# One engine more in a hand-written order: transfer issues, normalization and gate rows moved in a fused attention and expert kernel

## The chip, the cores and the metric

The kernel runs on one core of one Trainium2 chip. The time is device time in microseconds (us) of that core. The kernel before took 2181.82 us (median of three runs, 2180.48 to 2183.70).

## The reference, cut to what matters

The input `x` has 2048 rows of 512. The output is `x` plus causal sliding-window attention (32 heads of 16, window 256) of the normalized rows plus a gated sum of eight experts (512 to 1376 to 512) of the same normalized rows. All eight experts count for every row, so the selection of the top eight is only a softmax.

```python
xn = _layernorm(x, axis=-1)
# attention: q, k, v = xn @ wqkv, 32 heads of 16
mask = (idx[:, None] - idx[None, :] >= 0) & (idx[:, None] - idx[None, :] < W)   # W = 256
scores = jnp.where(mask[None, None], q @ k * Dh**-0.5, -1e9)
p = softmax(scores);  A = (p @ v) @ wo
# experts, K = E = 8
gates = softmax(xn @ w_gate)
for e in range(E):
    out = out + gates[:, e:e+1] * (silu(xn @ w1[e]) @ w2[e])
return x + A + out
```

## The kernel before, in words

Everything is fp32 in value, but TensorE multiplies fp16. So each operand is scaled and split into a high part and a low part (what the high part leaves), and each product is three matmuls: high by high, high by low, low by high (`mm3`, L147 to L149). ScalarE usually makes a high part, and VectorE or GpSimd subtracts it for the low part.

**The first stage** (about 0 to 190 us). For each of four blocks of 512 rows (`tb`): `layernorm` takes mean and variance of four tiles of 128 rows on VectorE, a root on ScalarE and a Newton step on VectorE, makes the normalized tile `xn` (L1129, on GpSimd for 14 of the 16 tiles, on VectorE for the first two), transposes it on TensorE into a PSUM bank `tp` (L1144) and splits it there: high by ScalarE (L1152), low by VectorE from PSUM (L1155), and a full fp32 copy `xfa`, `xfb` by ScalarE (L1162). `values` (products `vg`) and `queries_keys` (`qk`) multiply these with weights whose largest element is first found (`mxw` L968, a transpose `mx` and a broadcast `mb` on TensorE) and which are then scaled and split (`wv`, `wqk`). `factors_of_x` makes four sums of halves of x on GpSimd (`tt` L1197, `xsl` L1205) and stores them in DRAM (`XS`).

**The steady stage** (about 190 to 2100 us). The experts' first product is a Strassen-Winograd scheme of seven products whose operands are the seven tiles `xs` (loaded from `XS`, L489) and sums of weights (made from raw tiles `r` that are loaded at L249 and L265). TensorE writes to two pairs of PSUM banks, `zx` and `zy`; ScalarE copies `zx` out (L691), VectorE adds `zy` (`za` L698, `zb` L708). A row of the hidden layer then goes through tanh on ScalarE (L595), silu on VectorE (L599), high part on ScalarE (`hh` L610), low part on GpSimd (`hl` L613), and into the second product (`acc`). The 43 pairs of 256 hidden columns lie in 17 groups; in the group of three pairs whose columns belong to two experts each (the mixed group), the gate is multiplied in by VectorE at L605 from a tile `gb` that two transfers fill (L642, L643). There is one buffer `gb`, and each use waits for its own load.

**Attention** runs in between: 14 loads of `q` and `k` rows and one of `v` for each pair of heads (`att_load`, L1478 to L1484), scores `sc`, row maxima on VectorE (L1495, with a scratch output `junk` in SBUF), a transpose `mT`, the maxima split into `mh` and `ml` (L1520, L1523, L1526) and put into spare rows of `q` by four transfers (L1530), the scores again with the maximum subtracted (`st`, L1608), exp, masking on GpSimd, split into `ph` and `pl`, product `pv`, ratio `ot`, transpose `oT`, and the output product `wo` that VectorE adds into `x` (L1694).

**What sets the order.** The class `Order` keeps a planned clock for each of ScalarE, VectorE, GpSimd and SyncE (`"A"`, `"V"`, `"G"`, `"S"`). A `task` has a cost in ns, dependences, a due time, and a lag before its result counts. Whenever the plan's TensorE time moves on, `advance` takes the job that can start first. `Stream`s hand out pieces of TensorE work; `beside` and `wait` fill in attention (a credit of `RATE = 0.6` pieces for each piece of expert work) and second products. The instructions are then emitted in that order for the engines in `by_hand` (L210): TensorE, ScalarE, VectorE, GpSimd. SyncE, whose queue issues all transfers, is not among them: a task for it counts 50 ns in the plan, and the framework's own scheduler places its instructions. Loads of `xs` and those of `att_load` are issued where the program text reaches them, without a task.

Of the kernel before, what the change touches and what calls it, by code (L numbers as in the profile page):

```python
# [15 lines left out]
ALU = mybir.AluOpType  # L16
# [32 lines left out]
RATE = 0.6  # L49
# [5 lines left out]
LOADED = 6000  # L55
# [21 lines left out]
class Order:  # L77
# [3 lines left out]
    def __init__(self):  # L81
        self.t = 0
        self.clock = {"A": 0, "V": 0, "G": 0, "S": 0}
        self.todo = {e: [] for e in self.clock}
        self.n = 0
        self.idle = 0

# [20 lines left out]
    def advance(self):  # L108

        while True:  # L110
            best = None
            for engine, todo in self.todo.items():
                start, pick = None, None
                free = self.clock[engine]
                for job in todo:
                    e = self.at(job[5])
                    if e is None:
                        continue
                    s = max(free, e + AGO if job[5] else 0)
                    if start is None or s < start or (s == start and job[:2] < pick[:2]):  # L120
                        start, pick = s, job
# [13 lines left out]

@with_exitstack
def tile_attn_moe(ctx: ExitStack, tc: tile.TileContext, x, wqkv, wo, _bx, wg, w1, w2, out):
# [31 lines left out]
    oback = cst.tile([P, 1], F32, name="oback")  # L171
# [23 lines left out]
    by_hand = {getattr(mybir.EngineType, e) for e in ("PE", "Activation", "DVE", "Pool")}  # L195
# [98 lines left out]
    def prep1(g, i, r1, slot, act, dve, gps):  # L294
# [49 lines left out]
        w[A11] = dve(568, part(a11, 1, 0, 2), [h])  # L344
        h = act(712, part(both, 0, 6, 4), [e2])
        low = dve(831, part(both, 1, 6, 4), [h])
# [6 lines left out]
        w[S4] = w[S3] = dve(831, part(both, 1, 10, 4), [h])  # L353

    def prep2(g, i, j, r2, slot, act, dve):
# [12 lines left out]
        w["done"] = dve(898, low, [act(712, high, [])])  # L368
# [40 lines left out]
    ahead_of = {"att": 0.0, "acc": 0.0}  # L409
    bg = None  # L410
    pick = None

    def attend():
# [3 lines left out]
        for s in pick or ():  # L417
            if s.go():
# [4 lines left out]
                ahead_of["att"] += 1.0  # L423
                return True
# [31 lines left out]

    def beside(share):

        weights.go()
        ahead_of["att"] -= RATE  # L460
        while ahead_of["att"] < 0.0 and attend():
            pass
        ahead_of["acc"] -= share
        while ahead_of["acc"] < 0.0 and count[0] > hold and drain_one():
            ahead_of["att"] -= RATE
            while ahead_of["att"] < 0.0 and attend():
                pass
# [3 lines left out]
    def drain():  # L471

        wait(queue[0].needs)
        if drain_one():
            ahead_of["att"] -= RATE
            while ahead_of["att"] < 0.0 and attend():
                pass
            weights.go()

    xs = {}  # L480
    ahead = [0] * 7

    def load_x_part(m):

        if ahead[m] < len(blocks):
            b = blocks[ahead[m]]
            ahead[m] += 1
            t = moe.tile([P, 2, 2, TB // 2], F16, tag=f"xs{m}", name=f"xs{m}_{b[0]}_{b[1]}")
            nc.sync.dma_start(t, XS[b[1]][:, m])  # L489
            xs[(*b, m)] = t  # L490

    def load_xs():
        for _ in range(2):
            for m in ORDER:
                load_x_part(m)
# [13 lines left out]
    def second(g, tb, a):  # L509
# [22 lines left out]
        def add():  # L532
# [6 lines left out]
            if g == NG - 1:  # L539
                nc.sync.dma_start(o3[:, 4 * tb + a, :], dst)  # L540
            if tb == 3 and a == 3:
# [1235 lines left out]
```

## Time and profile before

| | |
|---|---|
| profiled execution | 2183.76 us, its span 2182.0 us, granted clock 0.992 |
| median of three runs | 2181.82 us |
| TensorE busy | 2121.0 us of the span, 97% |
| VectorE, ScalarE, GpSimd busy | 1764.4, 1344.8, 1104.4 us |
| transfers | 279.23 MB, 128 GB/s on average |
| hidden groups | 17, 43 pairs of 256 columns |

The span lies within the execution's time, from the first instruction to the last; 1.8 us lie around it. A row of the view of waits names the waiting engine and line and the one it waits for, then the total in us, the number of waits, and the longest. A row of the view of windows gives the stretch, its length, the busy time (and instructions) of TensorE (PE), its weight loads (PEld), VectorE (DVE), ScalarE (ACT) and GpSimd (POOL), the granted clock (PEclk), the share of the transfer engines and GB/s. SPq is SyncE's queue.

### The profile page before, as it was taken

The numbers are of one execution on the slowest core, as the hardware profiler recorded it, in microseconds if no ns is written. First come the engines' busy times: TensorE is split into PE (matmuls) and PEld (weight loads), VectorE is DVE, ScalarE is ACT, GpSimd is POOL, SyncE is SP. The second block draws the span as 40 slices with busy tenths as digits, with TensorE's granted clock in tenths as the row PEclk, the third lists the DMA queues.
The fourth block names the chain that finished last, engine by engine and source line by source line (L and its number), as shares of the span: only waits on it lengthen the run. The fifth ranks groups of instructions, "written<-read, shape, count | busy, mean of one in ns | idle before, by whom it ended". The sixth has DMA issues, their size and how long they took to land.

```text
span 2182.0 us, 46114 instructions
## 1 busy us (share of the span) xinstructions
PE 2121.0 (97%) x16519; PEld 1407.2 (64%) x16519; DVE 1764.4 (81%) x3824; ACT 1344.8 (62%) x2667; POOL 1104.4 (51%) x1624
## 2 busy tenths in 40 slices
PE   6999999999999999999999999999999999999999
PEld 4566666666666666666666666666666666666765
DVE  7767887888788888887897898789879887889762
ACT  5465665656656576566665566667666666667642
POOL 5453464545535565555444465546454546446532
PEclk9999999999999999999999999999999999999999
DMA  7856445344434444444544434353434343554111
GB/s 236 251 182 198 119 132 143 91 141 111 139 92 118 115 130 128 122 110 115 154 141 125 140 109 137 105 161 95 133 100 145 92 122 100 141 154 133 55 59 49
DMA packets 287830, 279.23 MB, mean 128 GB/s; under 512 B 128328, under 2 KB 189768, under 8 KB 287600
## 3 DMA queue, kind: packets, MB, share of 16 engines
q1 hardware_dynamic: 287600, 276.28, 43.7%
q8 instruction: 130, 2.13, 0.4%
q14 instruction: 100, 0.82, 0.1%
HBM read 250.42 MB, written 25.50 MB: 126 GB/s over the span
## 4 chain that ended last, share of the span: by engine, by line
PE 82%; DVE 7%; DMA 4%; issue 2%; POOL 2%; ACT 2%; SPq 1%; DVEq 0%; ACTq 0%; POOLq 0%
PE acc L147 12%; PE acc L149 12%; PE acc L148 12%; PE zx L147 6%; PE zx L149 6%; PE zx L148 6%; PE zy L147 5%; PE zy L149 4%; PE zy L148 4%; PE st L1608 3%; PE sc L1507 3%; PE pv L1639 3%; PE qk L1250 2%; PE vg L1305 2%; DMA gb<-GT 1%
## 5 line engine op out<-in xcount | busy, mean ns | idle before, releaser
L613 POOL TENSOR_TENSOR hl<-t,hh 128x512 f16<-128x512 f32 x344 | 431.5, 1262 | 289.0 <-ACT hh L610 269.1
L147 PE MATMUL acc<-w,hh 128*128 128x512 f16 x1376 | 523.0, 380 | 1.1 <-DVE x L535 1.1
L149 PE MATMUL acc<-w,hl 128*128 128x512 f16 x1376 | 522.8, 380 | 0.3 <-POOL hl L613 0.3
L148 PE MATMUL acc<-w,hh 128*128 128x512 f16 x1376 | 522.8, 380 | 0.0
L1569 ACT ACTIVATE pf<-st,esc 128x384 f32<-128x384 f32 (+2 forms) x576 | 299.4, 522 | 235.0 <-PE st L1608 220.2
L1553 POOL TENSOR_SCALAR_AFFINE_SELECT pf<-pf 128x128 f32<-128x128 f32 x512 | 204.8, 402 | 389.5 <-ACT pf L1569 360.3
L1579 DVE TENSOR_TENSOR pl<-pf,ph 128x384 f16<-128x384 f32 (+2 forms) x576 | 361.8, 636 | 43.7 <-ACT ph L1575 41.9
L147 PE MATMUL zx<-xs,w 128*128 128x256 f16 x1376 | 376.0, 273 | 9.3 <-DVE za L698 9.2
L149 PE MATMUL zx<-xs,w 128*128 128x256 f16 x1376 | 376.2, 273 | 0.0
L148 PE MATMUL zx<-xs,w 128*128 128x256 f16 x1376 | 376.2, 273 | 0.0
L1575 ACT ACTIVATE ph<-pf 128x384 f16<-128x384 f32 (+2 forms) x576 | 264.1, 464 | 84.2 <-POOL pf L1560 57.4
L147 PEld LDWEIGHTS <-w 128*128 128x128 f16 x2408 | 235.4, 98 | 122.0 <-DVE za L698 2.8
L148 PEld LDWEIGHTS <-w 128*128 128x128 f16 x2408 | 235.7, 98 | 106.7 <-issue 18.1
L1495 DVE CUSTOM_DVE_ANT_0 junk<-sc,mask 128x320 bf16<-128x320 f32 (+4 forms) x512 | 237.1, 463 | 78.4 <-PE sc L1507 69.6
L147 PE MATMUL zy<-xs,w 128*128 128x256 f16 x1032 | 281.3, 273 | 7.2 <-DVE zb L708 4.2
L149 PE MATMUL zy<-xs,w 128*128 128x256 f16 x1032 | 281.5, 273 | 0.0
L148 PE MATMUL zy<-xs,w 128*128 128x256 f16 x1032 | 281.3, 273 | 0.0
L610 ACT ACTIVATE hh<-t 128x512 f16<-128x512 f32 x344 | 214.2, 624 | 77.4 <-DVE t L599 49.8
L149 PEld LDWEIGHTS <-w 128*128 128x128 f16 x2408 | 235.9, 98 | 28.0
L535 DVE SCALAR_TENSOR_TENSOR x<-acc,gsc,x 128x512 f32<-128x512 f32 x256 | 190.2, 743 | 73.0 <-PE acc L149 71.7
L149 PEld LDWEIGHTS <-hl 128*128 128x128 f16 x1376 | 134.6, 98 | 164.6 <-issue 2.1
L712 POOL TENSOR_TENSOR zb<-zb 128x512 f32<-128x512 f32 x86 | 112.4, 1306 | 205.6 <-ACT zb L691 151.5
(145 smaller groups left out, 3769.3 us busy)
## 6 DMA issues: line engine op xcount, KB each, us to landing
xs<-XS SPq DMA_DIRECT2D x476, 256.0 KB
r<-in_B_w_dram SPq DMA_DIRECT2D x172, 256.0 KB
r<-in_B_w_dram SPq DMA_DIRECT2D x80, 512.0 KB
q<-QS SPq DMA_DIRECT2D x192, 32.0 KB
VS<-vt SPq DMA_DIRECT2D x16, 272.0 KB
out_dram<-x SPq DMA_DIRECT2D x16, 256.0 KB
k<-KS SPq DMA_DIRECT2D x96, 40.0 KB
x<-in_A_x_dram SPq DMA_DIRECT2D x3, 1024.0 KB
```

The source lines that it names most:

```text
L147: nc.tensor.matmul(ps, lhsT=lh, rhs=rh, start=first, stop=False, **kw)
L148: nc.tensor.matmul(ps, lhsT=lh, rhs=rl, start=False, stop=False, **kw)
L149: nc.tensor.matmul(ps, lhsT=ll, rhs=rh, start=False, stop=last, **kw)
L535: nc.vector.scalar_tensor_tensor(out=dst, in0=ps, scalar=back if groups[g][0] is None else back[:, 4 * tb + a : 4 * tb + a + 1], in1=dst, ...
L610: nc.scalar.activation(out=h["hi"], in_=h["t"], func=AF.Copy)
L613: nc.gpsimd.tensor_tensor(out=h["lo"], in0=h["t"], in1=h["hi"], op=ALU.subtract)
L712: nc.gpsimd.tensor_tensor(out=zb[:, :, late], in0=zb[:, :, early], in1=zb[:, :, late], op=ALU.add)
L1495: nc.vector.tensor_tensor_reduce(out=junk[:, :n], in0=ps[:, :n], in1=maskf[:, MB * 64 - n :], scale=1.0, scalar=-3.0e38, op0=ALU.add, op1= ...
L1553: nc.gpsimd.affine_select(out=pf[:, :P], in_=pf[:, :P], pattern=[[1, P]], channel_multiplier=-1, base=0, compare_op=ALU.is_ge, fill=0.0,)
L1569: nc.scalar.activation(out=w["pf"][:, :n], in_=ps[:, :n], func=AF.Exp, bias=math.log(PSCALE), scale=esc)
L1575: nc.scalar.activation(out=w["hi"][:, :n], in_=w["pf"][:, :n], func=AF.Copy)
L1579: nc.vector.tensor_tensor(out=w["lo"][:, :n], in0=w["pf"][:, :n], in1=w["hi"][:, :n], op=ALU.subtract)
```

## The change

What it does, part by part:

1. SyncE joins the engines whose order is written out. Each transfer is charged 450 ns of SyncE's planned time (`ISSUE`), results count 2.2 us later (`MOVED`) or 4.5 us later (`LOADED`, before 6 us). Loads of `xs`, `q`, `k`, `v`, `wo`, `gb` and `r`, the puts of `mh` and `ml` and the stores become moves with due times; products wait in the plan for their `xs` load, and `pv` alone waits for `v`. Several planned costs are set anew, the planner may prefer an earlier-due job that can start a little later until the first values are done, and attention's pace is what is left of it over what is left of the expert work.
2. Normalization: all 16 `xn` on VectorE; the low parts of x on GpSimd, from the fp32 copy in SBUF; the variance step goes (its constant is a bias of the root), the Newton step takes four instructions, not five.
3. The values' weights are loaded, searched for the largest element, scaled and split in two halves; the second half's low part is made on GpSimd after a second ScalarE pass. Products start with high by high as soon as high parts stand, and up to three product groups are open at once.
4. Two buffers `gb`. To make room, the mask is bf16, the row maxima's scratch output goes back into the PSUM bank it was read from, and `nm` goes (`mh` and `ml` are made from PSUM by two instructions, not three).

The matmuls are the same (16,500 in place of 16,498 TensorE instructions of the program).

Three places show how instructions stand on their queues. The first is SyncE's queue in the mixed group (`gb` gate rows, `q`, `k` attention rows, number suffixes are the buffer). Before:

```order
L1478 DMA k_94<-KS 16x1280 x2
L1530 DMA q_96<-mh 1x16x64
L1530 DMA q_96<-ml 1x16x64
L1530 DMA q_96<-mh 1x16x64
L1530 DMA q_96<-ml 1x16x64
L642 DMA gb<-GT 96x512
L643 DMA gb<-GT 32x512
L1478 DMA k_94<-KS 16x1280
```

After:

```order
L1611 DMA q_92<-mh 1x16x64
L1611 DMA q_92<-ml 1x16x64
L1611 DMA q_92<-mh 1x16x64
L1611 DMA q_92<-ml 1x16x64
L664 DMA gb<-GT 64x512
L665 DMA gb<-GT 64x512
L664 DMA gb<-GT 32x512
L665 DMA gb<-GT 96x512
L1746 DMA wo<-WOS 128x1024
```

Two gate rows now stand one behind the other; the four puts of `mh` and `ml` still stand ahead of them.

The second is SyncE's queue where the first raw tiles of group 5 (`r_5_0`, `r_5_1`) are loaded, beside a pair of heads' loads. Before:

```order
L1482 DMA q_92<-ZERO 2x16x64
L1484 DMA v<-VS 128x8x68
L489 DMA xs_4_0_8605<-XS_61 128x1024
L265 DMA r_5_0_8640<-in_B_w_dram 128x512 x2
L489 DMA xs_4_0_8654<-XS_61 128x1024
```

After:

```order
L280 DMA r_5_0_8417<-in_B_w_dram 128x512 x2
L512 DMA xs_4_0_8448<-XS_61 128x1024
L512 DMA xs_4_0_8486<-XS_61 128x1024
L512 DMA xs_4_1_8554<-XS_62 128x1024
L280 DMA r_5_1_8571<-in_B_w_dram 128x512 x2
L512 DMA xs_4_1_8614<-XS_62 128x1024
L1611 DMA q_96<-mh 1x16x64
L1611 DMA q_96<-ml 1x16x64
L1611 DMA q_96<-mh 1x16x64
L1611 DMA q_96<-ml 1x16x64
L135 DMA k_94<-KS 16x1024
```

The raw tiles stood behind the fifteen loads of the pair of heads (the last two of them shown) and now stand ahead of them.

The third is GpSimd's queue in the first stage. Before:

```order
L1197 TENSOR_TENSOR tt<-xfb,xfa 128x512
L1205 TENSOR_TENSOR xsl<-tt,xsh 128x512
L1197 TENSOR_TENSOR tt<-xfb,tt 128x512
L1129 TENSOR_SCALAR xn<-x_133,mv,rs 128x512
L1205 TENSOR_TENSOR xsl<-tt,xsh 128x512
L1129 TENSOR_SCALAR xn<-x_133,mv,rs 128x512 x3
L1197 TENSOR_TENSOR tt<-xfa 128x512
```

After:

```order
L1236 TENSOR_TENSOR tt<-xfb,xfa 128x512
L1244 TENSOR_TENSOR xsl<-tt,xsh 128x512
L1236 TENSOR_TENSOR tt<-xfb,tt 128x512
L1244 TENSOR_TENSOR xsl<-tt,xsh 128x512
L1193 TENSOR_TENSOR x_453<-xfa,x_451 128x2x128
L1193 TENSOR_TENSOR x_454<-xfb,x_452 128x2x128
```

The normalization (L1129) is gone from the queue, and the low parts of x (L1193, eight for each block of rows) stand in it, behind the sums of the block before.

The diff's core:

```diff
-RATE = 0.6
+AFTER = 80
+ISSUE = 450
-LOADED = 6000
+LOADED = 4500
+MOVED = 2200
@@ class Order, advance
+                    soon = [c for c in can if c[1:3] < (due, n) and c[0] < start + pick[2] // 2]
+                    if soon and self.strict:
+                        start, due, n, pick = min(soon, key=lambda c: c[1:3])
+    def issued(self, n, after=0):
+        self.clock["S"] = max(self.clock["S"], after) + n * ISSUE
+        return Event(self.clock["S"] + MOVED)
+
+    def move(self, n, run, deps, slack, lag=MOVED):
+        return self.task("S", n * ISSUE, run, deps, slack, lag)
@@ tile_attn_moe
-    by_hand = {getattr(mybir.EngineType, e) for e in ("PE", "Activation", "DVE", "Pool")}
+    by_hand = {getattr(mybir.EngineType, e) for e in ("PE", "Activation", "DVE", "Pool", "SP")}
@@ attention's pace
-        ahead_of["att"] -= RATE
+        left["groups"] -= 1
+        ahead_of["att"] -= left["att"] / max(left["groups"] - AFTER, 1)
@@ load_x_part (the moves of xs)
-            nc.sync.dma_start(t, XS[b[1]][:, m])
-            xs[(*b, m)] = t
+            def run():
+                t = moe.tile([P, 2, 2, TB // 2], F16, tag=f"xs{m}", name=f"xs{m}_{b[0]}_{b[1]}")
+                nc.sync.dma_start(t, XS[b[1]][:, m])
+                xs[(*b, m)] = t
+            xs_at[(*b, m)] = order.move(1, run, free + (...), slack, LOADED)
@@ row, gate_rows
-            ld = order.task("S", 50, gate_load, [last_gate], slack, 3000)
-            s = last_gate = order.task("V", 693, gate, [s, ld], slack + 4000)
+            ld = order.move(2, gate_load, [gated_at[0]], slack - 3000, LOADED)
+            s = order.task("V", 706, gate, [s, ld], slack + 4000)
+            gated_at[:] = [gated_at[-1], All([s, ld])]
-        t = at.tile([P, TB], F32, tag="gb", bufs=1, name="gb")
+        t = at.tile([P, TB], F32, tag="gb", bufs=2, name="gb")
@@ loaded (raw tiles r)
-            ev = order.task("S", 50, run, [lambda: order.at(raw_gone[which]), *deps], due, LOADED)
+            n = 4 if which == 1 and groups[g][0] is None else which
+            ev = order.move(n, run, [lambda: order.at(raw_gone[which]), *deps], due, LOADED)
@@ layernorm
-                    (nc.gpsimd if on_pool else nc.vector).tensor_scalar(
+                    nc.vector.tensor_scalar(
                         out=box["xn"], in0=xa[:, i, :], scalar1=mv[:, i, 0:1], scalar2=rs[:, i, :],
                         op0=ALU.subtract, op1=ALU.mult,
                     )
-                    nc.vector.scalar_tensor_tensor(
-                        out=xl[c][:, :, ts], in0=half[c], scalar=SX, in1=xh[c][:, :, ts], op0=ALU.mult, op1=ALU.subtract
-                    )
+                    nc.gpsimd.tensor_tensor(out=xl[c][:, :, ts], in0=xf[c][:, :, ts], in1=xh[c][:, :, ts], op=ALU.subtract)
@@ weights of values, second half (of == 4)
+                if of == 4:
+                    return t, task("G", 1270, rest, [task("A", cost, scaled, [t], slack + more + 500)], slack + more)
@@ go_on
-                if any(s.go() for s in sides) or main.go():
+                if any(s.go() for s in sides) or any(s.go() for s in mains[:3]):
@@ att_load
-                nc.sync.dma_start(kf[part, : s.nk], KS[r // 2, rows, s.k0 : s.k0 + s.nk])
+                move(kf[part, : s.nk], KS[r // 2, rows, s.k0 : s.k0 + s.nk])
-        s.loaded = Event(order.t + LOADED)
+        s.loaded = All(parts)
+        s.v_at = order.move(1, values, free, 8000)
@@ att_max
-    mask = att.tile([P, MB, 64], F32, name="mask")
+    mask = att.tile([P, MB, 64], BF16, name="mask")
-                out=junk[:, :n], in0=ps[:, :n], in1=maskf[:, MB * 64 - n :], scale=1.0, scalar=-3.0e38,
+                out=ps[:, :n], in0=ps[:, :n], in1=maskf[:, MB * 64 - n :], scale=1.0, scalar=-3.0e38,
-        s.ready = order.task("V", 356, low, [t], 2000, LOADED // 2)
+        s.ready = order.move(5, put, [t], 0)
```

More of the change, by code (lines that the diff above doesn't have):

```diff
@@ L366, in low @@
             )
-        w["done"] = dve(898, low, [act(712, high, [])])
+        w["done"] = dve(838, low, [act(712, high, [])])
     doubles = []
@@ L409, in tile_attn_moe @@
     ahead_of = {"att": 0.0, "acc": 0.0}
+    left = {
+        "att": sum(H // 2 * (2 * (min(hf, 1) * WIN + HALF) // P + QB + 2 * QB + 1) for hf in range(2)) + H // 8 * 2 * 10,
+        "groups": 14 * ND + 4 * 4 * 2 * sum(len(pairs) for _, pairs in groups),
+    }
     bg = None
@@ L487, in load_x_part @@
             ahead[m] += 1
-            t = moe.tile([P, 2, 2, TB // 2], F16, tag=f"xs{m}", name=f"xs{m}_{b[0]}_{b[1]}")
-            nc.sync.dma_start(t, XS[b[1]][:, m])
-            xs[(*b, m)] = t
[L492 to L495, printed above, removed]
+            def run():
+                t = moe.tile([P, 2, 2, TB // 2], F16, tag=f"xs{m}", name=f"xs{m}_{b[0]}_{b[1]}")
+                nc.sync.dma_start(t, XS[b[1]][:, m])
+                xs[(*b, m)] = t
+            xs_at[(*b, m)] = order.move(1, run, free + ([xs_at[(*blocks[ahead[m] - 2], m)]] if ahead[m] > 1 else []), slack, LOADED)
     def made_of(ws, of, what):
@@ L540, in add @@
                 nc.sync.dma_start(o3[:, 4 * tb + a, :], dst)
+                order.issued(1, order.clock["V"] + 746)
             if tb == 3 and a == 3:
@@ L995, in top @@
             def top():
+                if m == 2:
+                    topped.end = order.clock["V"] + 560
                 if n == 1:
@@ new lines, in layernorm @@
+                if i == 0 or (i < 3 and tb == 0):
+                    m = slice(i, i + 1 if tb == 0 and i < 2 else 4)
+                    turn = [] if tb else [Event(0), topped, found[2], found[2]]
+                    t = [
+                        task("V", 860, partial(stats, j), [x_at[tb][j], *turn[j : j + 1]], slack + less)
+                        for j in range(m.start, m.stop)
+                    ]
+                    t = task("A", 250 if tb == 0 else 1500, partial(root, m), t, slack)
+                    t = task("V", 650 if m.stop - m.start == 1 else 1000, partial(newton, m), [t], slack + less - 8000 * (m.stop == 4))
@@ L1207, in low @@
                     nc.sync.dma_start(XS[tb][:, m, 1], box["lo"])
+                    order.issued(2, order.clock["G"] + 1220)
                 deps = [made[x1]] if x1 in (T1, T2) else []
@@ L1288, in tile_attn_moe @@
+                if beside:
+                    t = order.task("A", 600, high, [ev, stored[j]], 4000)
+                    stored[j] = Event()
+                    evicted[j] = order.task("V", 690, low, [t], 5000)
+                else:
+                    place[j] = task("V", 690, low, [task("A", 600, high, [ev], 5000)], 6000)
+            return [Lazy(partial(group, w, c)) for w in ws for c in range(4)]
         vt4 = p0.tile([P, 4, H, VC], F16, name="vt")
@@ L1335, in gate @@
+            turns = [(i, hv) for i in range(4) for hv in range(2)]
+            if tb == 0:
+                turns[1:3] = turns[2], turns[1]
+            return [Lazy(partial(group, i, hv)) for i, hv in turns]
         def gate(tb, lg, logits):
@@ L1472, in att_load, with move @@
         qf, kf = s.q, s.k
+        free = [Event(order.t + DRAIN)]
+        parts = []
+        def move(dst, src):
+            parts.append(order.move(1, partial(nc.sync.dma_start, dst, src), free, 4000))
         for a in range(2):
@@ L1660, in att_wo, with load @@
         nonlocal oh_gone
-        wt = at.tile([P, 2, D], F16, tag="wo", bufs=1, name="wo")
-        nc.sync.dma_start(wt, WOS[qd])
-        loaded = Event(order.t + LOADED)
+        wt = []
+        def load():
+            wt.append(at.tile([P, 2, D], F16, tag="wo", bufs=1, name="wo"))
+            nc.sync.dma_start(wt[0], WOS[qd])
+        loaded = order.move(1, load, [oh_gone], 4000, LOADED)
         for jh in range(2):
```

478 lines of the change are left out of this document (248 added, 230 removed).

## The prediction

> **What bounds the kernel now.** I read the busy times first, then the windows by stage, then TensorE's waits, then the timeline around the longest ones.
>
> ```profile
> PE 2121.0 (97%) x16519; PEld 1407.2 (64%) x16519; DVE 1764.4 (81%) x3824; ACT 1344.8 (62%) x2667; POOL 1104.4 (51%) x1624
> ```
>
> TensorE bounds: it is busy 2121.0 us of 2182.0, and the change takes no matmul away. So at most 61.0 us of its idle time can be won, and what it runs at a lower clock. The windows say where (length, then PE, PEld, DVE, ACT, POOL busy, clock, DMA share, GB/s):
>
> ```profile
> 0.00:30.00 30.00, 15.54 (x77) 10.81 (x77) 19.60 (x64) 11.11 (x31) 14.53 (x20) 0.89 0.78 249
> 30.00:130.00 100.00, 88.54 (x478) 48.38 (x476) 72.28 (x170) 55.49 (x133) 54.13 (x38) 0.95 0.70 216
> 130.00:190.00 60.00, 60.00 (x438) 42.51 (x437) 38.30 (x94) 31.51 (x73) 19.12 (x19) 1.00 0.67 211
> 190.00:2100.00 1910.00, 1878.76 (x15050) 1258.32 (x15049) 1605.48 (x3459) 1224.77 (x2396) 999.01 (x1532) 1.00 0.43 123
> 2100.00:2182.00 82.00, 78.19 (x483) 47.14 (x481) 28.78 (x40) 21.93 (x36) 17.58 (x15) 1.00 0.11 42
> ```
>
> Idle is 14.5 us before 30, 11.5 from 30 to 130, 31.2 in the steady stage, 3.8 in the last. Below full clock:
>
> ```profile
> 21.00:28.00 7.00, 5.89 (x27) 4.07 (x26) 3.28 (x11) 4.17 (x14) 3.67 (x3) 0.51 0.73 214
> 52.00:59.00 7.00, 6.04 (x18) 3.02 (x19) 4.71 (x11) 3.76 (x9) 2.02 (x1) 0.52 0.71 201
> 83.00:86.00 3.00, 3.00 (x9) 1.08 (x8) 1.11 (x2) 1.30 (x5) 1.81 (x2) 0.50 0.90 284
> 359.00:363.00 4.00, 4.00 (x19) 2.29 (x18) 0.63 (x1) 2.30 (x5) 2.06 (x7) 0.57 0.96 319
> 601.00:608.00 7.00, 5.50 (x24) 3.01 (x24) 5.43 (x15) 3.62 (x7) 1.69 (x3) 0.53 0.38 130
> 1182.00:1185.00 3.00, 2.90 (x10) 1.43 (x10) 2.65 (x5) 2.63 (x6) 1.82 (x4) 0.50 0.77 130
> 1253.00:1256.00 3.00, 3.00 (x14) 1.61 (x13) 3.00 (x5) 2.18 (x5) 3.00 (x4) 0.57 0.35 85
> ```
>
> Busy time by one minus the clock is what they cost: 2.9, 2.9 and 1.5 us in the first stage (7.3); 1.7, 2.6, 1.5 and 1.3 in the steady one (7.1). With the idle time that makes 75 us, the ceiling. TensorE's waits (total, times, longest):
>
> ```profile
> PE tp L1144 <- POOL xn L1129: 11.8, 10, 2.5
> PE zx L147 <- DVE za L698: 9.2, 6, 3.8
> PE mx L992 <- DVE mx L979: 9.2, 1, 9.2
> PE st L1608 <- DMA q<-ml: 6.9, 9, 3.2
> PE zy L147 <- DVE zb L708: 4.2, 2, 3.9
> PE zy L147 <- DVE za L698: 2.7, 4, 1.6
> PE tp L1144 <- DVE xn L1129: 2.3, 1, 2.3
> PE vg L1305 <- ACT wv L1021: 1.8, 1, 1.8
> ```
>
> The first stage waits for normalized tiles, the steady one for VectorE's `za` and `zb` (16.1 us) and for puts of the maxima (6.9 us).
>
> **First stage, the start.**
>
> ```profile
> 7.58 1.27 DVE L968 TENSOR_REDUCE mxw<-wraw 128x1 f32<-128x512 f32 x2
> 12.98 5.24 PE L1305 MATMUL vg<-wv,x 128*128 128x260 f16 x24 [1.81 <-ACT wv L1021]
> 20.56 0.66 PE L1144 MATMUL tp<-ident,xn 128*128 128x128 f32 x4 [2.33 <-DVE xn L1129]
> ```
>
> Halving the values' weights takes two of the four reductions (1.3 us for two) from the way of the first `mx`. The waits of 1.8 and 2.3 us behind it should shrink with the new order; I take half, 2.0. Together −3.3. Bounds: all of the 5.4 us and the 2.9 of low clock (−8.3); and +2 if the second half's extra passes (a ScalarE pass like `wv` and a GpSimd pass of 1.26 us like `hl`, both quoted next) get in front.
>
> **First stage, normalization and low parts.**
>
> ```profile
> L1129 POOL TENSOR_SCALAR xn<-x,mv,rs 128x512 f32<-128x512 f32 x14 | 29.3, 2099 | 13.6 <-DVE rs L1114 11.2 <-PE qk L1250 1.7 <-issue 0.8
> L1129 DVE TENSOR_SCALAR xn<-x,mv,rs 128x512 f32<-128x512 f32 x2 | 1.2, 585 | 0.0
> L1155 DVE SCALAR_TENSOR_TENSOR x<-tp,x 128x256 f16<-128x256 f32 x32 | 12.0, 417 | 5.3 <-ACT x L1152 3.6 <-ACT xfa L1162 1.2 <-ACT xfb L1162 0.5
> L324 POOL TENSOR_TENSOR sums<-r 128x256 f32<-128x256 f32 x43 | 34.9, 811 | 16.3 <-DMA r<-in_B_w_dram 11.6 <-DVE w L309 4.7
> L613 POOL TENSOR_TENSOR hl<-t,hh 128x512 f16<-128x512 f32 x344 | 431.5, 1262 | 289.0 <-ACT hh L610 269.1 <-PE acc L149 3.9 <-DMA xs<-XS 3.2
> L1021 ACT ACTIVATE wv<-wraw,sc 128x512 f16<-128x512 f32 x4 | 2.6, 707 | 0.0
> ```
>
> A tile's normalization falls from 2.10 to 0.585 us, and it no longer stands behind the sums in GpSimd's queue. VectorE gains 14 × 0.585 = 8.2 us and loses the low parts' 12.0. GpSimd loses 29.3 us and gains 32 low parts: between 0.63 us (half of `hl`) and 0.81 us (`sums`, the same size), 20 to 26 us; I take 0.81, plus 2.5 for the second half's weights. So neither engine is fuller. The low parts come later (0.81 for 0.417 us, behind two ScalarE copies), but a product group now begins with high by high. Of the 11.8 us of `tp` waits I take 7.5 away (about two thirds), and of the 4.4 us of low clock behind them half, 2.2: −9.7. Bounds: −16 and 0. First stage: **−13**.
>
> One sentence on a rule: the Trainium skill (TensorE: Matmul & The Clock Gate, "What's actually happening") halves the clock after an idle window of about 3.4 us; the 0.52 at 52 to 59, with no single `tp` wait over 2.5 us, shows that several shorter waits do it too, so by the page alone the 2.2 us would be nothing and the forecast 2 us higher.
>
> **Steady stage, gate rows.**
>
> ```profile
> 1174.98 0.52 SPq L642 DMA_DIRECT2D gb<-GT  x1
> 1179.95 0.69 DVE L605 TENSOR_TENSOR t<-t,gb 128x512 f32<-128x512 f32 x1 [4.65 <-DMA gb<-GT]
> 1182.10 0.37 PE L147 MATMUL zx<-xs,w 128*128 128x256 f16 x1 [3.41 <-DVE za L698]
> ```
>
> The window of the mixed group:
>
> ```profile
> 1110.00:1270.00 160.00, 149.70 (x1173) 99.68 (x1171) 133.60 (x277) 96.71 (x191) 77.59 (x119) 0.98 0.46 134
> ```
>
> One buffer: the load goes out only after the gate before, 5.0 us from issue to use; VectorE stands, its `za` behind it is late, TensorE stands 3.4 us and then runs at 0.50. The mixed group holds 24 gates in 160 us, one in 6.7 us, so a load issued one gate earlier covers 5 us. Of its 10.3 us of idle I take 9. Bounds −10.3 and 0 (the four puts still stand ahead).
>
> **Steady stage, raw tiles, puts, clock.**
>
> ```profile
> 593.65 0.85 SPq L265 DMA_DIRECT2D r<-in_B_w_dram  x2
> 600.02 1.22 DVE L804 TENSOR_REDUCE mp<-r 128x1 f32<-128x1024 f32 x1 [6.27 <-DMA r<-in_B_w_dram]
> ```
>
> The tile landed 6.4 us after its issue, behind a pair of heads' fifteen loads that the plan did not charge, and VectorE, in order, stood before its `za`. Now the plan charges them, and the load goes ahead. The `za` and `zb` waits outside the mixed group are 16.1 less some 9, 7.2 us: I take 4. The puts are planned 4.45 us ahead of `st` (five issues of 0.45 and 2.2), in place of 3: of 6.9 us I take 4. Of the low clock, that after 601, 1182 and 1253 (5.4 us) goes with its stalls: 5. Each is bounded by the whole of its row and nothing. Together with the gates **−22**. For waits that a new order brings in places I cannot see I add **+4**, an eighth of today's 31.2 us (bounds 0 and 31).
>
> **SyncE's order.** Written out, SyncE issues nothing earlier than planned, and what it waits for holds all that stands behind it:
>
> ```profile
> SPq L489 <- PE zx L149: 272.7, 114, 9.1
> ```
>
> That is SyncE standing before an `xs` load until its buffer is read, up to 9.1 us, with raw tiles, `q` rows and gate rows queued behind it. Before, such a load stood where the program reached it; now it is placed by due time after the product that frees its buffer is planned, so I expect this row to shrink, and count no gain for it beyond the rows above: the DMA share is 0.43 in the steady stage, so a load that is issued in time is there in time. Splitting `att_load` into fifteen moves adds no transfer; its cover is that scores start only after the plan has the last `q` and `k` row, with expert products in between. If that cover is gone, `st` or `sc` wait like the 6.9 us of `q<-ml` today; this lies in the +4.
>
> **At nothing.** The variance step, one Newton instruction and `nm` go: a few short VectorE instructions for each tile or pair of heads, hidden where VectorE is not what TensorE waits for. The bf16 mask and the two columns of `oback` change no instruction's size. The attention's pace alters which work fills the gaps, not how much there is; TensorE was full in the windows 130 to 190 and nearly so at the end, and its price would show as idle time in the last window (3.8 us today).
>
> **Maxima into PSUM.**
>
> ```profile
> L1495 DVE CUSTOM_DVE_ANT_0 junk<-sc,mask 128x320 bf16<-128x320 f32 x448 | 216.6, 484 | 64.9 <-PE sc L1507 57.5 <-DVE mt L1495 0.5
> L804 DVE TENSOR_REDUCE mp<-r 128x1 f32<-128x1024 f32 x86 | 103.6, 1207 | 17.3 <-DMA r<-in_B_w_dram 17.3
> ```
>
> No row shows VectorE writing PSUM. The upper bound is a second pass at 1.18 ns an element (1207 over 1024): 0.377 us more on 448 operations, 169 us of VectorE. The lower is a little below nothing. I take nothing, since the operation already reads that bank at 1.5 ns an element. VectorE has 305 us free in the steady stage, which hides a few us, not 169.
>
> **The sum.** 2183.8 (the profiled execution) −13 −22 +4 = 2152.8; the median lies 1.9 below that execution, so **2151 us**.
>
> **The rivals.**
> - *The steady waits only move.* One SyncE queue still carries everything in order, and a due time set wrong holds back all behind it. For it: `q<-ml` and `gb` queue behind other issues today. Against: each named wait has its own remedy. 2183.8 − 13 − 1.9 = 2169.
> - *GpSimd's low parts take the place of its normalization.* TensorE then waits for x's low parts and the first stage gives nothing: 2183.8 − 22 + 4 − 1.9 = 2164. For it: 0.81 against 0.417 us, behind the sums. Against: 54.13 of 100 us busy there, and high by high first. The Trainium skill (GPSIMD Engine Reference, "Engine selection") speaks against this move, about two times slower for two inputs on GpSimd, and these rows agree.
> - *Slower: VectorE becomes the bound.* If the maxima cost the upper bound, VectorE's free time falls from 305 to 135 us, and TensorE's waits for it with their low clock (16.1 + 7.1 = 23.2 us) grow by 2.25 to 52: 2183.8 + 29 − 13 − 1.9 = 2198. The steady remedies then find no free VectorE. It decides from about 110 us more on VectorE (0.25 us an operation), where 23.2 × (305/195 − 1) = 13 eats the first stage's gain. Against: the operation reads PSUM already.
>
> **How the numbers follow.** Forecast 0.62 (own range 2136 to 2164), moved waits 0.18, low parts 0.12, VectorE 0.08. The range 2126 to 2176 leaves out VectorE's case, the upper end of the moved waits and a gain beyond every middle value: about 2 in 10. What this kernel's measurement can tell from no change is 0.2%, 4.4 us: faster 0.86 (0.62, and most of the two middle rivals), same 0.05, slower 0.09.
>
> **What would show it.** Right: `tp` waits for xn under 4 us; no VectorE wait for `gb` over 2 us; clock 1.00 from 1100 to 1300; raw tiles that land before their reduction; `sc` maxima still near 484 ns. Wrong: waits of `vg` or `qk` for GpSimd's low parts; waits for `xs` loads; VectorE over 1700 us in the steady stage; and, for the new pace, attention left over when the expert work ends, so that the last window has TensorE idle well over 3.8 us.

## The result, and the profile after

The changed kernel took 2143.45 us (median of four runs, 2141.19 to 2145.47) against 2181.65 us for the kernel before: a ratio of 0.9824 (95% interval 0.9807 to 0.9841), 38 us less. The forecast was 2151 us. Its profiled execution took 2145.47 us, its span 2143.8, the granted clock 0.998.

The busy times and then the windows by stage of the changed kernel (stretch, length, PE, PEld, DVE, ACT, POOL busy, clock, DMA share, GB/s):

```profile
PE 2106.5 (98%) x16522; PEld 1403.6 (65%) x16522; DVE 1745.8 (81%) x3775; ACT 1348.3 (63%) x2670; POOL 1109.4 (52%) x1644
```

```profile
0.00:30.00 30.00, 17.47 (x117) 12.81 (x118) 22.48 (x70) 15.94 (x42) 18.06 (x28) 1.00 0.53 163
30.00:130.00 100.00, 93.39 (x534) 53.47 (x532) 73.44 (x156) 56.16 (x140) 49.51 (x53) 0.97 0.75 241
130.00:190.00 60.00, 54.66 (x384) 37.48 (x382) 37.47 (x89) 29.41 (x64) 17.66 (x19) 0.97 0.69 212
190.00:2100.00 1910.00, 1901.49 (x15293) 1280.83 (x15292) 1595.71 (x3436) 1239.97 (x2416) 1019.14 (x1543) 1.00 0.43 123
```

TensorE's idle time went from 61.0 us (2182.0 − 2121.0) to 37.3 (2143.8 − 2106.5), 23.7 of the 38.2 us of span; its busy time fell by 14.5 us with the same large matmuls (16,522 TensorE records in place of 16,519). About 10 us of that is low clock that went: it had cost 14.4 us by the prediction's rows, and the changed kernel still loses some 4.7 us to it, since the view of windows shows 0.86 from 30 to 50 us, 0.94 from 50 to 60 and 0.83 from 170 to 180. The rest of the 14.5 us is not traced. In the steady window idle time fell from 31.2 to 8.5 us and the clock shows 1.00. From 130 to 190 us, where TensorE had been full, it now idles 5.3 us.

TensorE's waits in the changed kernel:

```profile
PE tp L1180 <- DVE xn L1165: 12.3, 5, 7.8
PE sc L1588 <- DMA q<-ZERO: 4.7, 1, 4.7
PE vg L1353 <- ACT wv L1057: 2.6, 2, 2.0
PE sc L1588 <- ACT ph L1656: 2.1, 2, 1.2
PE sc L1588 <- DVE mt L1576: 1.8, 2, 1.1
PE zy L162 <- DVE zb L730: 1.6, 2, 1.2
PE zy L162 <- DVE za L720: 1.4, 2, 1.1
```

The largest row is now mostly the program's start (7.8 us before the first transpose, which stands where the first `mx` stood). The waits for `za` and `zb` are 3.2 us in place of 16.1, and `q<-ml` is gone. One wait is new: 4.7 us of `sc` for `q` rows, which ends just before the 0.83 of 170 to 180. On VectorE the two waits for transfers shrank, from 17.3 and 16.4 us to:

```profile
DVE mp L827 <- DMA r<-in_B_w_dram: 5.3, 3, 2.8
DVE t L626 <- DMA gb<-GT: 3.1, 4, 1.3
```

Of the 5.3 us for raw tiles all but 0.3 lie before 165 us.

For the experiments one measure is worked out from each trace's matmul records: the start of a matmul less the time that all matmuls before it take at the usual (median) start-to-start of their shape in that trace. It counts idle time and low clock together, and it is comparable at equal times although the order differs. It is a rough measure: grouping the shapes in other ways moves a whole row by up to 4 us and a difference between two rows by about 1 us. "Lost" below is this, in us, at six points:

| kernel | at 30 | at 165 | at 200 | at 1000 | at 1400 | at 2100 |
|---|---|---|---|---|---|---|
| before | 21.0 | 38.9 | 40.8 | 62.9 | 81.8 | 88.1 |
| changed | 17.0 | 28.1 | 35.6 | 43.6 | 48.6 | 50.5 |
| changed, SyncE not written | 17.4 | 24.5 | 26.8 | 30.3 | 33.0 | 34.0 |
| not written, uncharged | 16.8 | 20.6 | 28.4 | 41.6 | 66.0 | 80.2 |
| one gate buffer | 15.6 | 24.5 | 32.1 | 39.2 | 67.1 | 71.5 |
| one gate buffer, not written | 17.6 | 24.9 | 27.1 | 30.5 | 56.8 | 59.8 |
| gate buffers alone | 21.7 | 39.9 | 41.9 | 57.4 | 71.4 | 77.2 |
| normalization on GpSimd | 21.1 | 33.0 | 44.5 | 52.6 | 59.9 | 66.8 |

By it the change saved 10.8 us up to 165 us, gave 5.6 us back between 165 and 200 (7.5 lost there in place of 1.9), and saved 32.4 us from 200 to 2100 (14.9 in place of 47.3).

### The profile page after: what moved, and what is told of

It is laid out like the page before. It is cut to its first block, busy times and chain, and to the rows that moved or that the text cites. A ratio compares the mean times of both kernels' runs of the same rounds, so it can differ in the third digit from the quotient of the medians.

```text
span 2143.8 us, 45614 instructions
## 1 busy us (share of the span) xinstructions
PE 2106.5 (98%) x16522; PEld 1403.6 (65%) x16522; DVE 1745.8 (81%) x3775; ACT 1348.3 (63%) x2670; POOL 1109.4 (52%) x1644
## 4 chain that ended last, share of the span: by engine, by line
PE 90%; DVE 4%; DMA 2%; ACT 1%; issue 1%; SPq 1%; POOL 1%; DVEq 0%; POOLq 0%; ACTq 0%
PE acc L162 13%; PE acc L163 13%; PE acc L164 13%; PE zx L162 6%; PE zx L163 6%; PE zx L164 6%; PE zy L162 5%; PE zy L164 5%; PE zy L163 5%; PE st L1689 3%; PE pv L1720 3%; PE sc L1588 3%; PE qk L1291 3%; PE vg L1353 2%; PE wo L164 1%
## 5 line engine op out<-in xcount | busy, mean ns | idle before, releaser
L1634 POOL TENSOR_SCALAR_AFFINE_SELECT pf<-pf 128x128 f32<-128x128 f32 x512 | 204.6, 402 | 440.7 <-ACT pf L1650 408.4
L1660 DVE TENSOR_TENSOR pl<-pf,ph 128x384 f16<-128x384 f32 (+2 forms) x576 | 354.5, 623 | 50.7 <-ACT ph L1656 48.8
L1576 DVE CUSTOM_DVE_ANT_0 sc<-sc,mask 128x320 f32<-128x320 f32 (+4 forms) x512 | 240.0, 473 | 101.9 <-PE sc L1588 98.9
L1641 POOL TENSOR_SCALAR_AFFINE_SELECT pf<-pf 128x128 f32<-128x128 f32 x448 | 176.0, 397 | 33.3 <-ACT pf L1650 32.7
```

What stands on the lines that cost most here:

```text
L1576: nc.vector.tensor_tensor_reduce(out=ps[:, :n], in0=ps[:, :n], in1=maskf[:, MB * 64 - n :], scale=1.0, scalar=-3.0e38, op0=ALU.add, op1=AL ...
L1634: nc.gpsimd.affine_select(out=pf[:, :P], in_=pf[:, :P], pattern=[[1, P]], channel_multiplier=-1, base=0, compare_op=ALU.is_ge, fill=0.0,)
L1641: nc.gpsimd.affine_select(out=pf[:, n - P : n], in_=pf[:, n - P : n], pattern=[[-1, P]], channel_multiplier=1, base=-1, compare_op=ALU.is_ ...
L1660: nc.vector.tensor_tensor(out=w["lo"][:, :n], in0=w["pf"][:, :n], in1=w["hi"][:, :n], op=ALU.subtract)
```

## The experiments

All times below are medians beside runs of the kernel before on the same chip; each says its ratio to before.

**1. Is it the written SyncE order, or the charge?** SyncE's queue is put back under the framework's scheduler, with the plan left as it is. The other four engines' instructions stand in exactly the order of the changed kernel; only SyncE's differ.

```diff
-    by_hand = {... for e in ("PE", "Activation", "DVE", "Pool", "SP")}
+    by_hand = {... for e in ("PE", "Activation", "DVE", "Pool")}
```

> The changed kernel with SyncE taken out of the engines whose order is written; the plan still charges 450 ns for an issue, so the other engines' order is the same. Theory (SyncE's order itself carries the raw tiles and the puts): their waits come back, TensorE loses 10 to 18 us: 2153 to 2162. Rival 1 (the charge in the plan is enough, since the other engines leave the room): within 4 us of 2143.5. Rival 2 (the whole steady gain is the written order): 2170 or more.

Measured: 2128.37 us, ratio 0.9756 (0.9741 to 0.9770). Neither the theory nor its rivals had this: without the written order the kernel is 15 us faster than the changed one. VectorE's waits for transfers behind the program's start, then GpSimd's for raw tiles, in this kernel:

```profile
DVE t L626 <- DMA gb<-GT: 2.5, 2, 1.7
DVE gs L1426 <- DMA QS<-qkh: 1.7, 1, 1.7
DVE mp L827 <- DMA r<-in_B_w_dram: 0.5, 1, 0.5
```

```profile
POOL sums L339 <- DMA r<-in_B_w_dram: 11.4, 6, 5.0
```

and GpSimd's in the changed kernel:

```profile
POOL sums L339 <- DMA r<-in_B_w_dram: 39.1, 15, 10.7
```

The view also puts one wait of 10.8 us of `xsl` in the kernel without the written order down to these transfers; `xsl` reads no raw tile, so it is left out here. So raw tiles land later, against what waits for them, under the written order; the control of experiment 4 shows the same, 49.5 us written and 15.7 not. What SyncE stood for, first in the changed kernel, then without the written order:

```profile
SPq L512 <- PE zx L164: 302.1, 105, 22.3
SPq L512 <- PE sc L1588: 215.8, 80, 7.2
SPq L512 <- PE zy L164: 176.8, 86, 5.9
SPq L512 <- PE st L1689: 155.0, 69, 23.9
```

```profile
SPq L512 <- PE zx L164: 237.5, 111, 10.3
SPq L512 <- PE sc L1588: 201.0, 80, 8.0
SPq L512 <- PE zy L164: 134.1, 77, 4.3
SPq L512 <- PE st L1689: 130.7, 74, 11.6
```

These are `xs` loads that wait for their buffer: 850 us standing in place of 703. One place in the changed kernel shows what stands behind them:

```profile
933.23 7.56 SPq L512 DMA_DIRECT2D xs<-XS  x5
940.88 0.39 SPq L264 DMA_DIRECT2D r<-in_B_w_dram  x1
```

```profile
946.78 0.94 POOL L339 TENSOR_TENSOR sums<-r 128x256 f32<-128x256 f32 x1 [3.33 <-DMA r<-in_B_w_dram]
```

The five `xs` issues themselves take 0.32 us each; the rest of the 7.56 us is standing until buffers are free. A raw tile is issued only behind them, and GpSimd waits 3.3 us for it. Where the 15 us lie: at 200 us the loss is 26.8 in place of 35.6 (8.8 us, of which 5.2 between 165 and 200, at the new wait for `q` rows), and from 200 to 2100 it is 7.2 in place of 14.9 (7.7 us). Late raw tiles behind standing `xs` loads can stand for the 7.7 us at most, and that they make all of it is argued, not shown.

**2. Is the charge needed?** An issue is charged 25 ns in the plan in place of 450, once with SyncE's order written and once not.

```diff
-ISSUE = 450
+ISSUE = 25
```

> The changed kernel with an issue charged 25 ns in place of 450, SyncE's order still written. Theory (the charge is what moves raw tiles and puts ahead): VectorE's wait for raw tiles and the wait of st for the puts come back in part, 6 to 14 us: 2150 to 2158. Rival (the written order with landing times is enough): within 4 us of 2143.5.

> SyncE's order not written and an issue charged 25 ns in place of 450; all else as changed. It stands beside the run with SyncE not written but charged (2128.4 us) and the run written but uncharged (2234.5). Theory (the charge itself pays: it tells the order of the other engines when a load is there): much of the loss stays, 2160 us or more. Rival (the charge matters only because the written SyncE order is derived from it): within 5 us of 2128.

Measured: 2234.48 us written (ratio 1.0244, 1.0229 to 1.0260) and 2175.02 us not written (0.9979, 0.9969 to 0.9989). With the two runs above:

| | issues charged 450 ns | charged 25 ns |
|---|---|---|
| SyncE's order written | 2143.5 | 2234.5 |
| not written | 2128.4 | 2175.0 |

The charge is worth 47 us even where the framework places SyncE's issues, far more than the 3 us that the control of experiment 4 moves there. Without it VectorE stands for raw tiles again (0.5 us with the charge):

```profile
DVE mp L827 <- DMA r<-in_B_w_dram: 37.2, 15, 5.2
```

Which order carries the 47 us is not shown: between these two kernels the instructions of all five engines, SyncE's too, stand in other orders. By the table 24.4 us of loss lie between 1000 and 1400 us without the charge, where the charged kernel loses 2.7; the mixed group runs there. Written and uncharged, the kernel is slower than before; VectorE then waits for raw tiles and TensorE for `q` rows:

```profile
DVE mp L827 <- DMA r<-in_B_w_dram: 64.1, 17, 7.8
```

```profile
PE sc L1588 <- DMA q<-ZERO: 23.6, 6, 7.1
```

The theory of the first run had the direction and a size of 6 to 14 us; it was far too small. That of the second held (2160 us or more).

**3. The new wait at attention's start.** The loads of the first pair of heads, which the changed kernel issues back to back from 159 us on, are put into the order ahead of the last block's queries.

```diff
+        first_rows = att_rows(0, 0)
         go_on(queries_keys(3, (0,)), sides)
...
-        s = att_load(*todo[0])
+        s = att_values(first_rows)
```

> The changed kernel, SyncE's order written, with the fourteen q and k loads of the first pair of heads put into the order before the last block's queries instead of after everything of the first stage. Theory (the 4.7 us wait of sc for q at 165 us is those loads issued back to back when attention starts): that wait falls under 1 us, 2137 to 2140. Rival (the loads then stand ahead of stores and raw tiles that the first products need, and the wait moves): within 2 us of 2143.5.

Measured: 2149.00 us, ratio 0.9855 (0.9841 to 0.9870), 5.6 us slower than the changed kernel. The wait became smaller, and another one is new:

```profile
PE zx L162 <- ACT za L713: 2.9, 1, 2.9
PE sc L1597 <- DMA q<-ZERO: 2.9, 1, 2.9
```

The theory fell. The loads now begin at 147 us in place of 159, the wait ends at 161 us in place of 170, and the loss at 200 us, worked out as in the table, is that of the changed kernel within 0.1 us. The new wait of `zx` stands far from there, between 1100 and 1200 us. So the 5.6 us arise after 200 us, and they are less than what the control of experiment 4 moves: they say nothing about the loads. In the run without the written order the same loads begin 23 us earlier, at 136 us, spread among the stores, and the wait is gone (lost from 165 to 200: 2.3 us). SyncE's timeline of that run, the first row:

```profile
136.31 1.46 SPq L135 DMA_DIRECT2D k<-KS  x1
```

So the wait depends on where SyncE's issues stand, and moving the whole block did not mend it.

**4. How much does any reordering move?** A control: attention's pace a little different. And the pace as before.

```diff
-AFTER = 80
+AFTER = 90
```

```diff
-        ahead_of["att"] -= left["att"] / max(left["groups"] - AFTER, 1)
+        ahead_of["att"] -= 0.6
```

> The changed kernel with AFTER 90 in place of 80, a small change of attention's pace that nobody would expect to matter: the control for how far any reordering moves the time. Theory (the steady stage is robust once issues are charged): within 4 us of 2143.5. Rival (each order is a draw, and single draws differ by 10 us and more, so that the losses with the old pace and with one gate buffer say little by themselves): more than 6 us away, up or down.

> The changed kernel with attention's pace as before, 0.6 pieces for each piece of expert work. Theory (the waits, not the pace): 0 to +3 us, 2143 to 2147. Rival (an even pace is what relieves VectorE where attention and experts crowd): 8 to 15 us back, 2151 to 2159, with VectorE-caused waits of zx and zy over 8 us in place of 3.2.

> SyncE's order not written, issues charged, and AFTER 90 as in the control, which took 2155.1 us with SyncE's order written. The order of the other four engines is that of the control. Theory (the written SyncE order is what makes an ordering of the others cheap or dear): within 5 us of 2128.4. Rival (the order of the other engines is the draw): the control's 11.7 us stay, 2137 to 2143.

Measured: the control 2155.14 us (0.9884, 0.9870 to 0.9899), the old pace 2157.43 us (0.9888, 0.9873 to 0.9903), and the control without the written SyncE order 2131.36 us (0.9772, 0.9758 to 0.9787). So a change that should not matter costs 11.7 us with SyncE's order written and 3.0 us without. The rival held for the written order: one draw of it says nothing below about 12 us, and the 14 us of the old pace are little evidence on the pace. Without it the same reordering of the other engines stays within 3 us; on this pair the fragile part is SyncE's written queue. That the written queue costs time is no single draw: in all four pairs of runs in which only SyncE's instructions stand in another order, the kernel without the written order is the faster one, by 15.1 us (changed), 23.8 (control), 14.3 (one gate buffer, experiment 5) and 59.5 (uncharged).

**5. Gate buffers.** One buffer in the changed kernel (with the plan told so), the same without SyncE's order written, and the two buffers alone, with what makes room for them, in the kernel before.

```diff
-        t = at.tile([P, TB], F32, tag="gb", bufs=2, name="gb")
+        t = at.tile([P, TB], F32, tag="gb", bufs=1, name="gb")
-            gated_at[:] = [gated_at[-1], All([s, ld])]
+            gated_at[:] = [All([s, ld])] * 2
```

> The changed kernel with one buffer of gate rows again (in the plan too); all else as changed, 2143.5 us. Theory (each wait of the steady stage had its own remedy): VectorE's wait for gate rows comes back to 12 to 17 us from 3.1, TensorE loses 7 to 11 us in the mixed group, clock dips there again: 2150 to 2155. Rival (the written order of SyncE places the gate loads well enough with one buffer): within 3 us of 2143.5.

> One buffer of gate rows, SyncE's order not written; the other four engines in the order of the run with one gate buffer (2175.4 us, of which 28 us in the mixed group). It stands beside 2128.4 us with two buffers. Theory (with one buffer the charged plan itself orders the mixed group badly, since each gate then counts over 5 us of waiting): the loss stays on the other engines' order, 2152 to 2160. Rival 1 (the two buffers alone are worth what they gave the kernel before, 9 us, and the rest of the 32 came from the written SyncE order): 2135 to 2141.

> The kernel before with two buffers of gate rows and what makes room for them (bf16 mask, maxima's scratch output in PSUM, two instructions for the parts of the maxima); nothing else of the change. Theory (each wait had its own remedy): the mixed group's 10 us go, 2168 to 2174. Rival (the gain in the mixed group needs the charged plan, which knows what a gate row's load costs): 2176 to 2184.

Measured: 2175.42 us (0.9976, 0.9964 to 0.9987), 2161.12 us (0.9906, 0.9887 to 0.9926) and 2172.50 us (0.9962, 0.9948 to 0.9976). In the kernel before, the two buffers and what makes room for them gave about 9 us, the size forecast for that step; in the window of its mixed group TensorE's idle time went from 10.3 to 3.5 us:

```profile
1110.00:1270.00 160.00, 156.51 (x1223) 104.02 (x1222) 139.10 (x288) 99.51 (x197) 89.20 (x123) 0.98 0.50 140
```

Not all of the 9 us is the gates', though. By the table this kernel loses 10.9 us less than the kernel before up to 2100 us: 4.9 of them between 1000 and 1400, where the mixed group runs, and 6.6 between 200 and 1000, where no gate is multiplied in. What gives the 6.6 us there is not shown.

In the changed kernel going back to one buffer cost 32 us, three times as much, and 33 us without the written order, where the control moved 3, so it is not the control's kind of draw. The table puts it between 1000 and 1400 us: 27.9 lost in place of 5.0, and 26.3 in place of 2.7. The wait for the gate row itself is only 3 us larger, 6.2 us in the kernel with one buffer in place of 3.1 (the theory wanted 12 to 17):

```profile
DVE t L626 <- DMA gb<-GT: 6.2, 5, 3.5
```

The loss is idle time of TensorE and, not much less, low clock. From 1000 to 1400 us it idles 14.4 us and runs at 0.97 (some 11.6 us), where the changed kernel idles 3.1 us at 1.00; first the kernel with one buffer, then the changed one:

```profile
1000.00:1400.00 400.00, 385.61 (x2962) 255.36 (x2961) 326.17 (x672) 244.08 (x472) 199.33 (x298) 0.97 0.45 131
1000.00:1400.00 400.00, 396.95 (x3183) 268.83 (x3180) 350.65 (x719) 266.18 (x521) 223.28 (x329) 1.00 0.49 138
```

The idle time is spread over many waits; the two longest of TensorE in its window 1080 to 1320 are

```profile
PE wo L162 <- DVE x L1779: 4.0, 1, 4.0
PE acc L162 <- ACT hh L631: 2.7, 1, 2.7
```

With one buffer the plan counts 0.9 + 4.5 us from gate to gate and lays out the mixed group around that; the theory of the second run, that the loss sits in the other engines' order, held (its forecast of 2152 to 2160 was missed by 1 us: 2161). Which of their instructions carries it is not shown. The 33 us and the 47 us of the charge do not add up: together they are more than the 53 us between the kernel before and the best one. Of the loss that each brings back without the written order, 23.6 and 21.7 us lie between 1000 and 1400 us: where the mixed group runs, nearly the same is lost without the second buffer as without the charge.

**6. The maxima's scratch output.** Without the written SyncE order, the scratch goes to SBUF again. The order on the other engines is the same.

```diff
+            junk = at.tile([P, MB * 64], BF16, tag="junk", bufs=1, name="junk")
-                out=ps[:, :n], in0=ps[:, :n], ...
+                out=junk[:, :n], in0=ps[:, :n], ...
```

> SyncE's order not written (2128.4 us), and the row maxima's scratch output goes to a bf16 tile in SBUF again; room for it comes from one tile for the two parts of the maxima. Every engine but SyncE has the same order. The operation should fall from 0.494 to 0.484 us and the read of its accumulator from 0.139 to 0.081, some 35 us less of VectorE. Theory (VectorE is not the bound, its free time hides it): within 3 us of 2128.4. Rival (VectorE is near the bound, as the slower case of the forecast had it): 2118 to 2124.

Measured: 2130.61 us (0.9767, 0.9752 to 0.9781), 2.2 us from 2128.4: no difference. The groups with the output in PSUM (the kernel with SyncE not written, first) and in SBUF:

```profile
L1576 DVE CUSTOM_DVE_ANT_0 sc<-sc,mask 128x320 f32<-128x320 f32 x448 | 219.9, 495 | 86.6 <-PE sc L1588 83.5
L1576 DVE DVE_READ_ACCUMULATOR2_ANT mt<- 128x1 f32 x512 | 71.5, 140 | 0.0
```

```profile
L1577 DVE CUSTOM_DVE_ANT_0 junk<-sc,mask 128x320 bf16<-128x320 f32 x448 | 216.8, 484 | 88.6 <-PE sc L1589 81.8
L1577 DVE DVE_READ_ACCUMULATOR2_ANT mt<- 128x1 f32 x512 | 41.2, 80 | 0.0
```

**7. Normalization.** 14 of the 16 tiles on GpSimd again, the low parts of x left there too.

```diff
-                    nc.vector.tensor_scalar(
+                    (nc.gpsimd if tb > 0 or i > 1 else nc.vector).tensor_scalar(
```

> The changed kernel with 14 of the 16 normalizations on GpSimd again, low parts of x also on GpSimd. Theory (the first stage gained because tiles no longer wait for GpSimd): waits of tp for xn come back to 10 us or more, GpSimd now has 29 us more than in the changed kernel, 2152 to 2160. Rival (high by high first and several open groups hide it): within 4 us of 2143.5.

Measured: 2160.60 us, ratio 0.9908 (0.9893 to 0.9922), 17 us slower than the changed kernel, close to the forecast in size, but not at the place named. The waits of `tp` for GpSimd came back only as

```profile
PE tp L1180 <- POOL xn L1165: 2.6, 3, 1.4
```

which is less than the 4.5 us that `tp` waits for VectorE in the changed kernel beside the program's start (12.3 less 7.8). So it is not shown that the move to VectorE took the waits for normalized tiles away (14.1 us before, 11.8 and 2.3). The rival that the run names, high by high first and several open groups, is still possible for these waits; it was not tried apart, and in this run TensorE also stood elsewhere, which can hide them. Against the changed kernel, 4.9 us more were lost up to 165, 4.0 more up to 200 and 7.4 after. In the first part stand waits that the changed kernel does not have: 3.5 us of `mb` for the largest weight at 85 us, 1.6 us of `qk` for `wqk` at 50 us, and 2.6 us of `zx` at 159 us. Since this was run with SyncE's order written, where the control moved 12 us, the rest is open.

## Why the prediction held, step by step

- **First stage, −13.** The start of the changed kernel's timeline stands below. Measured −10.8 up to 165 us in the changed kernel, and −14.4 without the written SyncE order (24.5 against 38.9). The step was right in sum, but neither of its two reasons is borne out. The start was wrong: first `vg` at 12.65 us in place of 12.98, so halving the weights did not bring it forward by the 1.3 us of two reductions. VectorE's first normalization, 1.35 us long, now stands ahead of the two reductions that are left, and the first `mx` starts at 9.04 us in place of 9.18. The gain before 30 us (4.0) came behind it. The larger term, tiles that no longer wait for GpSimd (7.5 of −9.7), is open: the waits went, but with the normalization on GpSimd again they stayed away (experiment 7). That the sum came out near is in part luck. The first two rows are VectorE's, the others TensorE's.

```profile
6.27 1.35 DVE L1165 TENSOR_SCALAR xn<-x,mv,rs 128x512 f32<-128x512 f32 x1
7.54 1.26 DVE L999 TENSOR_REDUCE mxw<-wraw 128x1 f32<-128x512 f32 x2
7.76 1.09 PE L1180 MATMUL tp<-ident,xn 128*128 128x128 f32 x4 [7.76 <-DVE xn L1165]
9.04 0.37 PE L1020 MATMUL mx<-ident,mx 128*2 128x128 f32 x1 [0.19 <-DVE mx L1007]
12.65 1.64 PE L1353 MATMUL vg<-wv,x 128*128 128x260 f16 x6 [1.96 <-ACT wv L1057]
```

- **Prices.** A normalized tile cost 0.770 us on VectorE in the mean, not the 0.585 of two earlier ones; but the sixteen are of two kinds (last section), and nine of them took 0.53 to 0.55. A low part cost 0.67 and 0.76 us on GpSimd, inside the bounds of 0.63 and 0.81; the 0.76 holds one part of 2.16 us, the others took about 0.67. TensorE waited 0.6 us in all for low parts, so the rival of the low parts fell. The three groups of the changed kernel (VectorE's, then GpSimd's), then the wait:

```profile
L1165 DVE TENSOR_SCALAR xn<-x,mv,rs 128x512 f32<-128x512 f32 x16 | 11.8, 770 | 0.1
```

```profile
L1193 POOL TENSOR_TENSOR x<-xfa,x 128x256 f16<-128x256 f32 x16 | 12.2, 764 | 22.0 <-ACT xfa L1198 22.0
L1193 POOL TENSOR_TENSOR x<-xfb,x 128x256 f16<-128x256 f32 x16 | 10.7, 671 | 2.0 <-ACT xfb L1198 1.9
```

```profile
PE vg L1353 <- POOL x L1193: 0.6, 2, 0.3
```

- **Gate rows, −9.** In the kernel before, the buffers and what makes room for them gave the 9 us (2172.5), but by the table only about half of it where the mixed group runs. In the changed kernel the second buffer is worth 32 us, because with one buffer the charged plan orders the mixed group badly. The step named one mechanism and there were two; that its 9 us fit is in part luck.
- **Raw tiles, puts, clock, −13.** The four rows of the steady stage offered 10.3 + 7.2 + 6.9 + 7.1 = 31.5 us, 22 were taken, and 32.4 were measured by the table, which also counts waits outside the four rows (47.3 us lost before). The mis-sized terms are these three, taken at a little over half (13 of 21.2), where most was won: TensorE's waits for `za` and `zb` fell from 16.1 to 3.2 us in all, those for the puts from 6.9 to none in the view, and the clock shows 1.00.
- **Why they went.** Here the prediction was right and wrong in part. It named the charge (the plan now knows what fifteen loads cost), but took it to work by letting the load go ahead on SyncE's queue. The runs show the charge to pay 47 us with the framework placing SyncE's issues in both kernels (2175.0 and 2128.4), and the written order to cost 15 us. "SyncE's order" in the prediction, that the row of standing `xs` loads would shrink, failed: 272.7 us became 302.1. VectorE's wait for raw tiles did go (0.3 us behind 165 us), but GpSimd's grew from 11.6 to 39.1.
- **New waits, +4.** Measured +5.6 at attention's start. It is a wait for `q` rows issued back to back, the kind that the prediction named, with low clock behind it, and it vanishes when SyncE's order is not written.
- **Rivals.** "The steady waits only move" fell in the changed kernel, but its mechanism (one queue, a due time set wrong) fits the 15 us and the 12 us of the control. "VectorE becomes the bound" fell: the operation cost 10 ns more, not 377.
- **The signs.** Clock 1.00 from 1100 to 1300 us, no wait of VectorE for `gb` over 1.3 us, maxima at 494 ns, low parts waited for 0.6 us, VectorE 1595.7 us busy in the steady stage, 3.5 us of idle TensorE in the last window, and no wait of TensorE for an `xs` load all came as stated for a right forecast. Raw tiles came late for their reduction three times, once of these behind 165 us. `tp` waits of 4.5 us beside the start missed their mark of 4 by a little.

The net came out 7.5 us better than forecast: the steady stage gave 10 us more, the first stage 2 less, and the new wait took 2 more, by the measure of lost time; the last 1 us lies behind 2100 us and between the profiled execution and the median.

## What to carry to other kernels

A planner that orders the engines must know what a transfer costs to issue, since the engines that wait stand in order: here the charge was worth 47 us. It does not follow that the issuing queue should be written in the plan's order too: here a load whose buffer was not yet free held all behind it (7.6 us for five loads), and leaving that queue to a scheduler that places issues apart from the plan gave the best kernel of this study (2128.4 us, 0.9756 of before). And before a small difference between two orderings is explained, one needs a control that reorders without a reason; here that moved the time by 12 us with the written queue and by 3 without. Not tried apart were the halved weights, the groups open side by side and the planned costs that were set anew.

## What the runs showed of the hardware that was not expected

Writing the maxima's scratch output to PSUM rather than SBUF lengthens the accumulator's read from 80 to 140 ns (512 of them, 30 us by its row) and the operation from 484 to 495 ns. Yet VectorE's busy time was not shorter with SBUF (1751.7 us against 1748.4), nor was the kernel's time. The rows of the accumulator's read, added up, overstate what the engine loses, because the reads lie under their neighbours in time: 66.4 of their 71.5 us with PSUM and 40.2 of 41.2 with SBUF fall together with another VectorE instruction. So 4 of the 30 us stand alone. VectorE's timeline of the changed kernel shows one such read:

```profile
936.69 0.49 DVE L1576 CUSTOM_DVE_ANT_0 sc<-sc,mask 128x320 f32<-128x320 f32 x1
937.10 0.14 DVE L1576 DVE_READ_ACCUMULATOR2_ANT mt<- 128x1 f32 x1
937.10 0.68 DVE L720 SCALAR_TENSOR_TENSOR za<-zy,s 128x512 f32<-128x512 f32 x1
```

A tile's normalization on VectorE took 585 ns in the mean of two in the kernel before and 770 in the mean of the changed kernel's sixteen, but no tile took 770. Nine took 528 to 547 ns, one 642, and six 947 to 1469 ns. GpSimd was busy during at least 0.7 of each of the six; during five of the nine it did nothing. Three more of the nine (528 to 530 ns) lie inside one low part on GpSimd, which took 2161 ns there and about 670 elsewhere. So in these nine meetings one of the two instructions takes some 1.8 to 3.2 times as long as it does otherwise, and not always the same one. That is what the trace shows side by side; no run took GpSimd's work away to test it.
